# Dense layer with squared ReLU: a new order of loads and transposes in the head of the kernel

## The chip, the cores and the metric

The kernel runs on one core of a Trainium2 chip. The metric is the time of one execution on the device in microseconds, as the median of several runs. A core has a matrix engine (TensorE, called PE in the profile, with its weight loads as PEld), VectorE (DVE), ScalarE (ACT), GpSimd (POOL) and SyncE (SP), and 16 DMA engines[...]. The queues used here are those of SyncE (`nc.sync`), ScalarE (`nc.scalar`) and GpSimd (`nc.gpsimd`). SBUF is the working memory with 128 partitions; PSUM holds what TensorE writes, in eight banks.

## What is computed

Two dense layers with a squared ReLU between them, all in bfloat16:

```python
B, S, D, F = 1, 2048, 576, 4608
h = jnp.einsum("bsd,df->bsf", x, w1) + b1
r = jnp.where(h > 0, h, 0)
h = r * r
out = jnp.einsum("bsf,fd->bsd", h, w2) + b2
```

The width D = 576 is four full chunks of 128 and a rest of 64. This rest, the "tail columns" of x and the "small rows" of w1, is what makes the head of the kernel intricate.

## The kernel before

The 2048 rows of x are cut into four blocks of 512. For each block the first layer needs x transposed (the width on the partitions). Blocks 1 to 3 come transposed by DMA; block 0 is loaded as it is, in four tiles of 128 rows, and transposed by TensorE, so that work can start early. The columns of w1 are split: the first 512 (4 groups of 128, tile `w1n`, 128 rows at a time, and `w1n8` for the last 64 rows) are used in block 0 at once; the other 4096 (`w1_h`) are used in `a_rows`, in pairs of products that fill the upper and the lower half of the array with 64 rows each. For these, the transposed x (`xT`) holds every 64-row chunk in both partition halves: nine slots named `E3, O, .., SPC, E, ..`, filled by copies between the halves (`dup_windows`).

The head, in program order. First the warm-up products and the loads:

```python
wps = ps_o.tile([P, 512], FP32, name="wps", tag="po")
WARM = [512] * 6 + [128]
for i, n in enumerate(WARM):
    keep(nc.tensor.matmul(wps[:, 0:n], lhsT=ones[:, 0:P], rhs=ones[:, 0:n], start=True, stop=True))
...
def load_x(eng, rt):                                    # one tile of 128 rows, 144 KB
    keep(eng.dma_start(out=xs[:, rt, :], in_=x2[rt * P:(rt + 1) * P, :]))
def load_w1n(eng, k):                                   # 128 rows x 512 columns, 128 KB
    keep(eng.dma_start(out=w1n[:, k, :], in_=w1[k * P:(k + 1) * P, 0:GW]))
def load_w1n8(eng, h):                                  # 64 rows, 2 of the 4 groups, 32 KB
    src = w1[NK * P:D, 0:GW].rearrange("p (i h f) -> p i h f", h=2, f=P)
    keep(eng.dma_start(out=w1n8[h * H:(h + 1) * H, :, :], in_=src[:, :, h, :]))
...
load_x(nc.sync, 0)
load_x(nc.scalar, 1)
load_w1n(nc.sync, 0)
load_x(nc.scalar, 2)
load_w1n(nc.sync, 1)
load_x(nc.sync, 3)
for k in range(2, NK):                                  # NK = 4
    load_w1n(nc.sync, k)
...                                                     # b1 and b2 by GpSimd's queue
for (j0, j1) in [(0, 1), (1, 2), (2, 4), (4, 6), (6, 8), (8, 10), (10, 12)]:
    load_w1(nc.sync, 0, j0, j1)                         # w1_h: 144 KB for one j, 288 KB for two
    load_w1(nc.sync, 1, j0, j1)
    if j0 == 0:
        load_w1n8(nc.sync, 0)
        load_w1n8(nc.sync, 1)
```

Then the transposes of block 0, its copies out of PSUM, and the first products. `part(h, k)` is four products (one for each group) of chunk k with the half h of the block (256 rows). `x_transpose(j, k)` is one transpose of tile j; k = 4 (NK) is the tail, taken as the last 128 columns.

```python
for j in range(2):
    for k in range(NK):
        x_transpose(j, k)
for j in range(2):
    x_transpose(j, NK)
x_copies(0)                          # PSUM to xT: 3 by VectorE, 2 by ScalarE
part(0, 0)
for k in range(NK + 1):
    x_transpose(2, k)
part(0, 1)
part(0, 2)
for k in range(NK + 1):
    x_transpose(3, k)
x_copies(1)
dup_windows(0)                       # two copies of 64 x 2048 by VectorE
part(0, 3)
part(1, 0)
make_b1T()                           # transposes b1 and copies it
for k in range(1, NK):
    part(1, k)
...
for i in (1, 0):                     # the small rows: pairs of products of 64 rows, then ReLU
    pair(i, False, True)
    ...
```

After the head come `a_rows(0)`, where each step j has 18 products in 9 pairs and takes two new PSUM banks, and the rest of the kernel, which the change hardly touches: the first layer of block 1, the last 128 output columns for both (`phase_t`), the others (`phase_b`), and the same for blocks 2 and 3.

Of the kernel before, what the change touches and what calls it, by code (L numbers as in the profile page):

```python
# [11 lines left out]
BF16 = mybir.dt.bfloat16  # L12
FP32 = mybir.dt.float32
# [4 lines left out]
def kernel(  # L18
# [21 lines left out]
    GW = G * P  # L40
# [18 lines left out]
    wps = ps_o.tile([P, 512], FP32, name="wps", tag="po")  # L59
    ones = nc.const_aps.tensor(1.0, [P, 512], BF16)  # L60
    WARM = [512] * 6 + [128]
    for i, n in enumerate(WARM):
        keep(nc.tensor.matmul(wps[:, 0:n], lhsT=ones[:, 0:P], rhs=ones[:, 0:n], start=True, stop=True))  # L63

    xs = const.tile([P, RT, D], BF16, name="x_sb")
    w1n = wpool.tile([P, NK, GW], BF16, name="w1n")
    w1n8 = wpool.tile([P, G // 2, P], BF16, name="w1n8")
    w1_h = wpool.tile([P, NC, FH], BF16, name="w1_h")
    w1_v = w1.rearrange("(c p) f -> p c f", p=H)

    def load_x(eng, rt):
        keep(eng.dma_start(out=xs[:, rt, :], in_=x2[rt * P:(rt + 1) * P, :]))

    def load_w1n(eng, k):
        keep(eng.dma_start(out=w1n[:, k, :], in_=w1[k * P:(k + 1) * P, 0:GW]))

    def load_w1n8(eng, h):
        src = w1[NK * P:D, 0:GW].rearrange("p (i h f) -> p i h f", h=2, f=P)
        keep(eng.dma_start(out=w1n8[h * H:(h + 1) * H, :, :], in_=src[:, :, h, :]))

    def load_w1(eng, h, j0, j1):
        keep(eng.dma_start(out=w1_h[h * H:(h + 1) * H, :, j0 * P:j1 * P],
                      in_=w1_v[:, :, GW + h * FH + j0 * P:GW + h * FH + j1 * P]))

    load_x(nc.sync, 0)
    load_x(nc.scalar, 1)
    load_w1n(nc.sync, 0)
    load_x(nc.scalar, 2)
    load_w1n(nc.sync, 1)
    load_x(nc.sync, 3)  # L90
    for k in range(2, NK):
        load_w1n(nc.sync, k)

    ident = const.tile([P, P], BF16, name="ident")
    make_identity(nc, ident[:])
    b1_rows = const.tile([P, P], BF16, name="b1_rows")
    nc.gpsimd.memset(b1_rows[:], 0.0)
    nc.gpsimd.dma_start(out=b1_rows[0:NFT, :], in_=b1.rearrange("(ft p) -> ft p", p=P))
    b2_col = const.tile([P, 1], BF16, name="b2_col")
    nc.gpsimd.dma_start(out=b2_col[:], in_=b2[DM:D].rearrange("(d o) -> d o", o=1))  # L100
    b2T = const.tile([P, 1], FP32, name="b2T")
    nc.gpsimd.tensor_copy(out=b2T[:], in_=b2_col[:])
    warm = const.tile([P, 1], FP32, name="warm")
    keep(nc.scalar.activation(out=warm[:], in_=nc.const_aps.tensor(0.0, [P, 1], FP32), func=ACT.Relu))

    E3, O, SPC, E = 0, 1, 5, 6
    LO_W = [O, O + 1, O + 2, O + 3, E, E + 1, E + 2, E3, SPC]
# [30 lines left out]
    alloc_xT(0)  # L138
    xT0 = xT_blk[0]
    HS = SB // 2  # L140
    tb_po = [ps_o.tile([P, 2, HS], BF16, name="tb", tag="po") for _ in range(2)]
    tb_ph = [ps_h.tile([P, 2, HS], BF16, name="tb", tag="ph") for _ in range(4)]
    half_banks = [tb_ph, None]

    def x_transpose(j, k):
        h, q = divmod(j, 2)
        qc = slice(q * P, (q + 1) * P)
        bank, slot, c0 = (half_banks[h][k], 0, k * P) if k < NK else (half_banks[h][2], 1, D - P)
        keep(nc.tensor.transpose(bank[:, slot, qc], xs[:, j, c0:c0 + P], ident[:]))  # L149

    def x_copies(h):
        hc = slice(h * HS, (h + 1) * HS)
        for k in range(NK):
            src = half_banks[h][k][:, 0, :]
            if k % 2 == 0:
                keep(nc.vector.tensor_copy(out=xT0[:, O + k, hc], in_=src))  # L156
            else:
                keep(nc.scalar.copy(out=xT0[:, O + k, hc], in_=src))
        keep(nc.vector.tensor_copy(out=xT0[:, E3, hc], in_=half_banks[h][2][:, 1, :]))


    b1T = const.tile([P, NFT], FP32, name="b1T")

    def make_b1T():
        b1T_ps = ps_o.tile([P, P], BF16, name="b1T_ps", tag="po")
        keep(nc.tensor.transpose(b1T_ps[:], b1_rows[:], ident[:]))  # L166
        keep(nc.vector.tensor_copy(out=b1T[:], in_=b1T_ps[:, 0:NFT]))

# [26 lines left out]
    def a_full(sb, order):  # L195
        xT = xT_blk[sb]
        banks = []
        for g in range(G):
            pool, tag = (ps_o, "po") if g < 2 else (ps_h, "ph")
            banks.append(pool.tile([P, SB], FP32, name="pn", tag=tag))  # L200

        def pair(i, start, stop):
            keep(nc.tensor.matmul(banks[2 * i][:], lhsT=w1n8[0:H, i, :], rhs=xT[0:H, SPC, :],  # L203
                             start=start, stop=stop, skip_group_check=order == "k_outer"))
            keep(nc.tensor.matmul(banks[2 * i + 1][:], lhsT=w1n8[H:P, i, :], rhs=xT[H:P, E3, :],  # L205
                             start=start, stop=stop, skip_group_check=order == "k_outer"))

        def full(g, k, start, stop):
            keep(nc.tensor.matmul(banks[g][:], lhsT=w1n[:, k, g * P:(g + 1) * P], rhs=xT[:, O + k, :],  # L209
                             start=start, stop=stop))  # L210

        if order == "rows_first":
            for i in (1, 0):
                pair(i, True, False)
            for g in (2, 3, 0, 1):
                for k in range(NK):
                    full(g, k, False, k == NK - 1)
                evac_h(sb, banks[g], g)
        else:
            if order == "k_outer":  # L220
                tb_new = [ps_h.tile([P, 2, HS], BF16, name="tb", tag="ph") for _ in range(2)]
                half_banks[1] = tb_new + tb_po

                def part(h, k):
                    hc = slice(h * HS, (h + 1) * HS)
                    for g in range(G):
                        keep(nc.tensor.matmul(banks[g][:, hc], lhsT=w1n[:, k, g * P:(g + 1) * P],  # L227
                                              rhs=xT[:, O + k, hc], start=(h == 0 and k == 0), stop=False,
                                              skip_group_check=True))

                for j in range(2):
                    for k in range(NK):
# [12 lines left out]
                dup_windows(0)  # L245
                part(0, 3)
                part(1, 0)
                make_b1T()
                for k in range(1, NK):
                    part(1, k)  # L250
            else:
                for g in (2, 3, 0, 1):
                    for k in range(NK):
                        full(g, k, k == 0, False)
            for i in (1, 0):
                pair(i, False, True)
                evac_h(sb, banks[2 * i], 2 * i)
                evac_h(sb, banks[2 * i + 1], 2 * i + 1)
# [35 lines left out]
    for (j0, j1) in [(0, 1), (1, 2), (2, 4), (4, 6), (6, 8), (8, 10), (10, 12)]:  # L294
        load_w1(nc.sync, 0, j0, j1)
        load_w1(nc.sync, 1, j0, j1)
        if j0 == 0:
            load_w1n8(nc.sync, 0)
            load_w1n8(nc.sync, 1)
    load_xT(1)  # L300
    for (j0, j1) in [(12, 14), (14, 16)]:
        load_w1(nc.sync, 0, j0, j1)
        load_w1(nc.sync, 1, j0, j1)
    keep(nc.sync.dma_start(out=b2_bc[:], in_=b2.partition_broadcast(P)))
    for c in (0, 2, 1, 3):
        load_w2(c)
    load_xT(2)

# [51 lines left out]
```

## Time and profile before

| what | value |
|---|---|
| time, median of 3 runs | 291.11 us (290.89 to 291.23) |
| span of the profiled run | 289.6 us |
| TensorE busy | 285.5 us, 2027 products |
| ScalarE, VectorE busy | 96.7 us, 78.6 us |
| x tile 0: issue, landing | 0.73 us, 3.72 us |
| first transpose of x | 3.77 us |
| first product of w1_h (start of `a_rows`) | 10.29 us |

How to read it: "busy" is the time during which an engine had an instruction under way. TensorE's instructions overlap, so the step from the start of one to the start of the next is the better measure of its speed. The chain of waits goes back from the last instruction to what released it, step by step; what lies on it sets the end. A time "to landing" goes from the issue of a transfer to its last completion mark[...]. The span begins about a microsecond before the kernel's first own instructions.

### The profile page before, as it was taken

The numbers are of one execution on the slowest core, as the hardware profiler recorded it, in microseconds if no ns is written. First come the engines' busy times: TensorE is split into PE (matmuls) and PEld (weight loads), VectorE is DVE, ScalarE is ACT, GpSimd is POOL, SyncE is SP. The second block draws the span as 40 slices with busy tenths as digits, with TensorE's granted clock in tenths as the row PEclk, the third lists the DMA queues.
The fourth block names the chain that finished last, engine by engine and source line by source line (L and its number), as shares of the span: only waits on it lengthen the run. The fifth ranks groups of instructions, "written<-read, shape, count | busy, mean of one in ns | idle before, by whom it ended". The sixth has DMA issues, their size and how long they took to land.

```text
span 289.6 us, 4693 instructions
## 1 busy us (share of the span) xinstructions
PE 285.5 (99%) x2027; PEld 139.9 (48%) x2032; DVE 78.6 (27%) x176; ACT 96.7 (33%) x154; POOL 2.3 (1%) x10
## 2 busy tenths in 40 slices
PE   8999999999999999999999999999999999999996
PEld 5544444444444555555544444444444455555555
DVE  1644554444500200000015444444440001100001
ACT  2566666666500000000027666666670000000000
POOL 3000000000000000000000000000000000000000
PEclk9999999999999999999999999999999999999999
DMA  7999999400001200000000000000000110000000
GB/s 198 221 245 188 308 389 212 92 0 2 0 14 25 52 16 18 16 16 18 16 16 2 1 2 0 2 0 2 0 2 0 36 38 16 16 16 19 33 16 18
DMA packets 31605, 16.52 MB, mean 57 GB/s; under 512 B 15700, under 2 KB 31584, under 8 KB 31584
## 3 DMA queue, kind: packets, MB, share of 16 engines
q1 hardware_dynamic: 31232, 15.91, 22.3%
q10 hardware_dynamic: 288, 0.30, 0.4%
q8 instruction: 16, 0.26, 0.4%
q14 instruction: 5, 0.04, 0.0%
q0 software_dynamic: 64, 0.01, 0.0%
HBM read 11.36 MB, written 2.36 MB: 47 GB/s over the span
## 4 chain that ended last, share of the span: by engine, by line
PE 98%; DMA 1%; issue 0%; DVE 0%
PE ph L188 42%; PE po L289 38%; PE pt L270 11%; PE pn L209 4%; PE pn L227 1%; DMA x_sb<-in_x_dram 1%; PE tb L149 1%; PE ph L190 1%; PE pn L203 1%; DVE o_sb L291 0%; PE b1T_ps L166 0%; PE pn L205 0%
## 5 line engine op out<-in xcount | busy, mean ns | idle before, releaser
L190 PE MATMUL ph<-xTw,w_h 64*128 64x512 bf16 x576 | 124.6, 376 | 0.0
L188 PE MATMUL ph<-xTw,w_h 64*128 64x512 bf16 x576 | 124.6, 376 | 0.0
L289 PE MATMUL po<-w_sb,hT 128*128 128x448 bf16 (+2 forms) x612 | 109.4, 341 | 0.0
L176 ACT ACTIVATE r<-ph,b1T 128x512 bf16<-128x512 f32 x128 | 81.1, 685 | 41.6 <-PE ph L190 41.6
L188 PEld LDWEIGHTS <-w_h 64*128 64x128 bf16 x576 | 54.1, 94 | 68.3
L289 PEld LDWEIGHTS <-hT 128*128 128x128 bf16 x612 | 58.5, 98 | 51.0
L177 DVE TENSOR_TENSOR hT<-r 128x512 bf16<-128x512 bf16 x144 | 61.2, 426 | 75.9 <-ACT r L176 75.5
L190 PEld LDWEIGHTS <-w_h 64*128 64x128 bf16 x576 | 54.1, 94 | 0.0
L291 DVE TENSOR_TENSOR o_sb<-po,b_bc 128x448 bf16<-128x448 f32 (+2 forms) x17 | 10.2, 597 | 125.8 <-PE po L289 125.8
L270 PE MATMUL pt<-hT,w_sb 128*128 128x512 bf16 x142 | 31.3, 379 | 0.1
L176 ACT ACTIVATE r<-pn,b1T 128x512 bf16<-128x512 f32 x16 | 10.3, 688 | 61.0 <-PE pn L205 59.6
L270 PEld LDWEIGHTS <-w_sb 128*128 128x128 bf16 x144 | 14.1, 98 | 17.0
L273 ACT ACTIVATE oT<-pt,b2T 128x512 bf16<-128x512 f32 x4 | 2.8, 688 | 28.3 <-PE pt L270 28.3
L209 PE MATMUL pn<-xTw,w1n 128*128 128x512 bf16 x45 | 10.4, 379 | 0.4 <-issue 0.3
L209 PEld LDWEIGHTS <-w1n 128*128 128x128 bf16 x48 | 4.5, 98 | 6.0 <-issue 0.8
L227 PE MATMUL pn<-xTw,w1n 128*128 128x256 bf16 x32 | 4.6, 295 | 0.0
L63 PE MATMUL wps<-const-bfloat16-1.0 128*128 128x512 bf16 (+1 forms) x7 | 2.8, 582 | 0.8 <-PEq L344 0.8
L227 PEld LDWEIGHTS <-w1n 128*128 128x128 bf16 x32 | 3.3, 107 | 0.5
L156 DVE COPY xTw<-tb 128x256 bf16<-128x256 bf16 x4 | 1.1, 292 | 6.7 <-PE tb L149 6.7
L119 DVE COPY xTw<-xTw 64x2048 bf16<-64x2048 bf16 x4 | 2.8, 690 | 0.2
L120 DVE COPY xTw<-xTw 64x2048 bf16<-64x2048 bf16 x4 | 2.7, 687 | 0.1
L149 PE MATMUL tb<-ident,x_sb 128*128 128x128 bf16 x20 | 2.4, 288 | 0.2 <-DMA x_sb<-in_x_dram 0.2
(23 smaller groups left out, 15.2 us busy)
## 6 DMA issues: line engine op xcount, KB each, us to landing
w_sb<-in_w_dram SPq DMA_DIRECT2D x4, 1296.0 KB, 12.7
w_h<-in_w_dram SPq DMA_DIRECT2D x14, 288.0 KB, 6.2
out_dram<-o_sb SPq DMA_DIRECT2D x15, 112.0 KB, 1.7
w_h<-in_w_dram SPq DMA_DIRECT2D x4, 144.0 KB, 3.5
w1n<-in_w_dram SPq DMA_DIRECT2D x4, 128.0 KB, 3.9
out_dram<-ot SPq DMA_DIRECT2D x4, 128.0 KB, 2.0
x_sb<-in_x_dram ACTq DMA_DIRECT2D x2, 144.0 KB, 2.9
x_sb<-in_x_dram SPq DMA_DIRECT2D x2, 144.0 KB, 3.4
```

What stands on the lines that cost most here:

```text
L63: keep(nc.tensor.matmul(wps[:, 0:n], lhsT=ones[:, 0:P], rhs=ones[:, 0:n], start=True, stop=True))
L149: keep(nc.tensor.transpose(bank[:, slot, qc], xs[:, j, c0:c0 + P], ident[:]))
L176: keep(nc.scalar.activation(out=r[:], in_=bank[:], func=ACT.Relu, bias=b1T[:, ft:ft + 1], scale=1.0))
L177: keep(nc.vector.tensor_tensor(out=hTs[sb][:, ft, :], in0=r[:], in1=r[:], op=ALU.mult))
L188: keep(nc.tensor.matmul(bx[:], lhsT=w1_h[0:H, LO_C[i], jc], rhs=xT[0:H, LO_W[i], :], start=(i == 0), stop=(i == NC - 1)))
L190: keep(nc.tensor.matmul(by[:], lhsT=w1_h[H:P, UP_C[i], jc], rhs=xT[H:P, UP_W[i], :], start=(i == 0), stop=(i == NC - 1)))
L203: keep(nc.tensor.matmul(banks[2 * i][:], lhsT=w1n8[0:H, i, :], rhs=xT[0:H, SPC, :], start=start, stop=stop, skip_group_check=order == "k_o ...
L209: keep(nc.tensor.matmul(banks[g][:], lhsT=w1n[:, k, g * P:(g + 1) * P], rhs=xT[:, O + k, :], start=start, stop=stop))
L227: keep(nc.tensor.matmul(banks[g][:, hc], lhsT=w1n[:, k, g * P:(g + 1) * P], rhs=xT[:, O + k, hc], start=(h == 0 and k == 0), stop=False, s ...
L270: keep(nc.tensor.matmul(pt[:], lhsT=w2_sb[:, ft, DM:D], rhs=hT[:, ft, :], start=(i == 0), stop=(i == NFT - 1)))
L289: keep(nc.tensor.matmul(po[:, 0:d1 - d0], lhsT=hT[:, ft, jj * P:(jj + 1) * P], rhs=w2_sb[:, ft, d0:d1], start=(i == 0), stop=(i == NFT - 1)))
L291: keep(nc.vector.tensor_tensor(out=o_sb[:, d0:d1], in0=po[:, 0:d1 - d0], in1=b2_bc[:, d0:d1], op=ALU.add))
```

## The change: what it does and what it is for

- One of the six long warm-up products is gone, and the warm-up writes to the other PSUM pool.
- Tile 0 of x is loaded in two column pieces, one on each queue, so that its first transposes can start with the first piece. All four tiles of x are asked for ahead of w1. The four chunks of w1n come in three loads, two of them on ScalarE's queue.
- The small rows of w1 come once in a single load that writes the same 64 rows to both partition halves (the source is read twice), instead of two loads that each bring half of the columns.
- All 16 full transposes of block 0 stand in front, in banks that hold two chunks each; VectorE does six of the eight copies.
- The tail columns (64 wide) of two x tiles are first put side by side by GpSimd, so that one transpose serves two tiles. These two transposes stand behind chunk 1 of the first half. Four small copies then take the tails to their places, and the two large copies between the halves become one of 64 x 2048 by VectorE, one of 64 x 512 by VectorE and one of 64 x 1536 by ScalarE.
- The four accumulators of the head all lie in one PSUM pool, those of the transposes in the other.
- b1 and b2 come by the hardware queues, b2's column much later; w2 comes in three loads in place of four.

The core of the diff:

```diff
-    WARM = [512] * 6 + [128]
+    WARM = [512] * 5 + [128]
...
-    w1n8 = wpool.tile([P, G // 2, P], BF16, name="w1n8")
+    w1n8 = wpool.tile([P, GW], BF16, name="w1n8")
...
+    def load_w1n8(eng):
+        src = w1[NK * P:D, 0:GW].unsqueeze(0).broadcast_to([2, H, GW])
+        keep(eng.dma_start(out=w1n8[:, :], in_=src))
...
-    load_x(nc.sync, 0)
-    load_x(nc.scalar, 1)
-    load_w1n(nc.sync, 0)
-    load_x(nc.scalar, 2)
-    load_w1n(nc.sync, 1)
-    load_x(nc.sync, 3)
-    for k in range(2, NK):
-        load_w1n(nc.sync, k)
+    load_x(nc.sync, 0, 0, 2 * P)
+    load_x(nc.scalar, 0, 2 * P, D)
+    load_x(nc.sync, 1)
+    load_x(nc.scalar, 2)
+    load_x(nc.sync, 3)
+    load_w1n(nc.scalar, 0, 1)
+    load_w1n(nc.sync, 1, 2)
+    load_w1n(nc.scalar, 2, NK)
...
+    load_w1n8(nc.sync)
+    keep(nc.scalar.dma_start(out=b1_rows[0:NFT, :], in_=b1.rearrange("(ft p) -> ft p", p=P)))
+    xs8 = const.tile([P, RT, H], BF16, name="xs8")
+    for h in range(2):
+        keep(nc.gpsimd.tensor_copy(out=xs8[:, 2 * h:2 * h + 2, :], in_=xs[:, 2 * h:2 * h + 2, NK * P:D]))
...
-    W2CH = 9
+    W2CH = 12
...
+    def dup_windows_first():
+        keep(nc.scalar.copy(out=xT0[0:H, E:E + 3, :], in_=xT0[H:P, O:O + 3, :]))
+
+    def transpose_tails():
+        tl = ps_h.tile([P, 2, P], BF16, name="tl", tag="ph")
+        for h in range(2):
+            keep(nc.tensor.transpose(tl[:, h, :], xs8[:, 2 * h:2 * h + 2, :], ident[:]))
+        x8 = xT0.rearrange("p c (h q t) -> p c h q t", h=2, q=2)
+        for q in range(2):
+            keep(nc.vector.tensor_copy(out=x8[H:P, E3, :, q, :], in_=tl[q * H:(q + 1) * H, 0:2, :]))
+        for q in range(2):
+            keep(nc.vector.tensor_copy(out=x8[0:H, SPC, :, q, :], in_=tl[q * H:(q + 1) * H, 0:2, :]))
+        keep(nc.vector.tensor_copy(out=xT0[H:P, SPC:SPC + 4, :], in_=xT0[0:H, O:O + 4, :]))
+        keep(nc.vector.tensor_copy(out=xT0[0:H, E3, :], in_=xT0[H:P, O + 3, :]))
...
-                for j in range(2):
-                    for k in range(NK):
-                        x_transpose(j, k)
-                for j in range(2):
-                    x_transpose(j, NK)
-                x_copies(0)
+                for j in range(RT):
+                    x_transpose(j)
+                dup_windows_first()
                 part(0, 0)
-                for k in range(NK + 1):
-                    x_transpose(2, k)
                 part(0, 1)
+                transpose_tails()
                 part(0, 2)
-                for k in range(NK + 1):
-                    x_transpose(3, k)
-                x_copies(1)
-                dup_windows(0)
                 part(0, 3)
-                part(1, 0)
-                make_b1T()
-                for k in range(1, NK):
+                for k in range(NK):
                     part(1, k)
+                    if k == 1:
+                        make_b1T()
...
-        if j0 == 0:
-            load_w1n8(nc.sync, 0)
-            load_w1n8(nc.sync, 1)
```

More of the change, by code (lines that the diff above doesn't have):

```diff
@@ L57 @@
     ps_o = ctx.enter_context(tc.tile_pool(name="ps_o", bufs=4, space=PSUM))
-    wps = ps_o.tile([P, 512], FP32, name="wps", tag="po")
+    wps = ps_h.tile([P, 512], FP32, name="wps", tag="ph")
     ones = nc.const_aps.tensor(1.0, [P, 512], BF16)
-    WARM = [512] * 6 + [128]
+    WARM = [512] * 5 + [128]
     for i, n in enumerate(WARM):
@@ L66, with load_x, load_w1n @@
     w1n = wpool.tile([P, NK, GW], BF16, name="w1n")
-    w1n8 = wpool.tile([P, G // 2, P], BF16, name="w1n8")
+    w1n8 = wpool.tile([P, GW], BF16, name="w1n8")
     w1_h = wpool.tile([P, NC, FH], BF16, name="w1_h")
     w1_v = w1.rearrange("(c p) f -> p c f", p=H)
[L71 to L79, printed above, removed]
+    def load_x(eng, rt, c0=0, c1=D):
+        keep(eng.dma_start(out=xs[:, rt, c0:c1], in_=x2[rt * P:(rt + 1) * P, c0:c1]))
+    def load_w1n(eng, k0, k1):
+        src = w1[k0 * P:k1 * P, 0:GW].rearrange("(k p) f -> p k f", p=P)
+        keep(eng.dma_start(out=w1n[:, k0:k1, :], in_=src))
+    def load_w1n8(eng):
+        src = w1[NK * P:D, 0:GW].unsqueeze(0).broadcast_to([2, H, GW])
+        keep(eng.dma_start(out=w1n8[:, :], in_=src))
     def load_w1(eng, h, j0, j1):
@@ L83, in load_w1 @@
                       in_=w1_v[:, :, GW + h * FH + j0 * P:GW + h * FH + j1 * P]))
-    load_x(nc.sync, 0)
-    load_x(nc.scalar, 1)
-    load_w1n(nc.sync, 0)
+    b1_rows = const.tile([P, P], BF16, name="b1_rows")
+    nc.vector.memset(b1_rows[:], 0.0)
+    load_x(nc.sync, 0, 0, 2 * P)
+    load_x(nc.scalar, 0, 2 * P, D)
+    load_x(nc.sync, 1)
     load_x(nc.scalar, 2)
-    load_w1n(nc.sync, 1)
     load_x(nc.sync, 3)
-    for k in range(2, NK):
-        load_w1n(nc.sync, k)
+    load_w1n(nc.scalar, 0, 1)
+    load_w1n(nc.sync, 1, 2)
+    load_w1n(nc.scalar, 2, NK)
     ident = const.tile([P, P], BF16, name="ident")
     make_identity(nc, ident[:])
[L96 to L102, printed above, removed]
     warm = const.tile([P, 1], FP32, name="warm")
     keep(nc.scalar.activation(out=warm[:], in_=nc.const_aps.tensor(0.0, [P, 1], FP32), func=ACT.Relu))
+    load_w1n8(nc.sync)
[3 more added lines that the diff above has]
+        keep(nc.gpsimd.tensor_copy(out=xs8[:, 2 * h:2 * h + 2, :], in_=xs[:, 2 * h:2 * h + 2, NK * P:D]))
     E3, O, SPC, E = 0, 1, 5, 6
@@ L140, with x_transpose @@
     HS = SB // 2
[L141 to L145, printed above, removed]
+    tb = [[ps_h.tile([P, 4, HS], BF16, name="tb", tag="ph") for _ in range(2)] for _ in range(2)]
+    def x_transpose(j):
         h, q = divmod(j, 2)
-        qc = slice(q * P, (q + 1) * P)
-        bank, slot, c0 = (half_banks[h][k], 0, k * P) if k < NK else (half_banks[h][2], 1, D - P)
-        keep(nc.tensor.transpose(bank[:, slot, qc], xs[:, j, c0:c0 + P], ident[:]))
@@ L151, in x_copies @@
-    def x_copies(h):
         hc = slice(h * HS, (h + 1) * HS)
-        for k in range(NK):
[L154 to L159, printed above, removed]
-    b1T = const.tile([P, NFT], FP32, name="b1T")
+        for bank in range(2):
+            for k in range(2 * bank, 2 * bank + 2):
+                keep(nc.tensor.transpose(tb[h][bank][:, k % 2, q * P:(q + 1) * P], xs[:, j, k * P:(k + 1) * P], ident[:]))
+            for k in range(2 * bank, 2 * bank + 2) if q == 1 else ():
+                copy = nc.scalar.copy if h == 1 and bank == 1 else nc.vector.tensor_copy
+                keep(copy(out=xT0[:, O + k, hc], in_=tb[h][bank][:, k % 2, :]))
@@ L164, in make_b1T @@
     def make_b1T():
-        b1T_ps = ps_o.tile([P, P], BF16, name="b1T_ps", tag="po")
+        b1T_ps = ps_h.tile([P, P], BF16, name="b1T_ps", tag="ph")
         keep(nc.tensor.transpose(b1T_ps[:], b1_rows[:], ident[:]))
@@ L198, in a_full @@
         for g in range(G):
-            pool, tag = (ps_o, "po") if g < 2 else (ps_h, "ph")
+            pool, tag = (ps_o, "po") if g < 2 or order == "k_outer" else (ps_h, "ph")
             banks.append(pool.tile([P, SB], FP32, name="pn", tag=tag))
         def pair(i, start, stop):
-            keep(nc.tensor.matmul(banks[2 * i][:], lhsT=w1n8[0:H, i, :], rhs=xT[0:H, SPC, :],
+            keep(nc.tensor.matmul(banks[2 * i][:], lhsT=w1n8[0:H, 2 * i * P:(2 * i + 1) * P], rhs=xT[0:H, SPC, :],
                              start=start, stop=stop, skip_group_check=order == "k_outer"))
-            keep(nc.tensor.matmul(banks[2 * i + 1][:], lhsT=w1n8[H:P, i, :], rhs=xT[H:P, E3, :],
+            keep(nc.tensor.matmul(banks[2 * i + 1][:], lhsT=w1n8[H:P, (2 * i + 1) * P:(2 * i + 2) * P], rhs=xT[H:P, E3, :],
                              start=start, stop=stop, skip_group_check=order == "k_outer"))
@@ L220, in a_full @@
             if order == "k_outer":
-                tb_new = [ps_h.tile([P, 2, HS], BF16, name="tb", tag="ph") for _ in range(2)]
-                half_banks[1] = tb_new + tb_po
                 def part(h, k):
@@ L229, in part @@
                                               skip_group_check=True))
-                for j in range(2):
-                    for k in range(NK):
-                        x_transpose(j, k)
-                for j in range(2):
-                    x_transpose(j, NK)
-                x_copies(0)
+                for j in range(RT):
+                    x_transpose(j)
+                dup_windows_first()
                 part(0, 0)
-                for k in range(NK + 1):
-                    x_transpose(2, k)
                 part(0, 1)
+                transpose_tails()
                 part(0, 2)
-                for k in range(NK + 1):
-                    x_transpose(3, k)
-                x_copies(1)
-                dup_windows(0)
                 part(0, 3)
-                part(1, 0)
-                make_b1T()
-                for k in range(1, NK):
+                for k in range(NK):
                     part(1, k)
+                    if k == 1:
+                        make_b1T()
             else:
@@ L303 @@
         load_w1(nc.sync, 1, j0, j1)
+    b2_col = const.tile([P, 1], BF16, name="b2_col")
+    keep(nc.sync.dma_start(out=b2_col[:], in_=b2[DM:D].rearrange("(d o) -> d o", o=1)))
+    b2T = const.tile([P, 1], FP32, name="b2T")
+    keep(nc.gpsimd.tensor_copy(out=b2T[:], in_=b2_col[:]))
     keep(nc.sync.dma_start(out=b2_bc[:], in_=b2.partition_broadcast(P)))
-    for c in (0, 2, 1, 3):
+    for c in range(3):
         load_w2(c)
```

## The prediction

> **What bounds the kernel now.** I read the page first (busy shares), then the chain of waits over the first 11 us, then the engines' busy time by stretch, then the issues of transfers with their time to landing. The page:
>
> ```profile
> PE 285.5 (99%) x2027; PEld 139.9 (48%) x2032; DVE 78.6 (27%) x176; ACT 96.7 (33%) x154; POOL 2.3 (1%) x10
> PE 98%; DMA 1%; issue 0%; DVE 0%
> ```
>
> TensorE is busy for 99% of the span, and 98% of the chain that ended last lies on it. So only two things count: how much TensorE has to do, and when it can start. The busy time by stretch (columns: stretch, its length, then busy time and instruction count of PE, PEld, DVE, ACT, POOL, clock, DMA share, GB/s) shows where idle time is left:
>
> ```profile
> 0.00:3.77 3.77, 2.83 (x7) 0.89 (x7) 0.00 (x0) 1.49 (x2) 2.07 (x9) 1.00 0.52 153
> 3.77:9.85 6.08, 6.08 (x54) 5.24 (x55) 2.97 (x9) 1.29 (x4) 0.18 (x1) 1.00 0.83 206
> 9.85:77.00 67.15, 66.99 (x603) 30.20 (x604) 31.60 (x74) 45.26 (x72) 0.00 (x0) 1.00 0.73 173
> ```
>
> From 9.85 us on TensorE has 66.99 us of work in 67.15: nothing to win there. The change touches only what lies ahead of it, the head: 3.77 us of which the 2.83 busy ones are warm-up products that nobody uses, and 6.1 us of transposes and first products. The chain of waits, in order of time (start us, length us, what):
>
> ```profile
> 0.73 2.99 DMA x_sb<-in_x_dram
> 3.73 0.04 issue
> 3.77 1.25 PE tb L149 x10
> 5.02 0.86 PE pn L227 x4
> 5.88 0.53 PE tb L149 x5
> 6.42 0.98 PE pn L227 x8
> 7.40 0.28 PE tb L149 x5
> 7.68 0.87 PE pn L227 x8
> 8.55 0.06 PE b1T_ps L166
> 8.61 1.31 PE pn L227 x12
> ```
>
> Three readings. First, the head waits for x tile 0 until 3.72 us (0.73 + 2.99), though the last warm-up product, which the timeline starts at 3.29, has left TensorE free from about 3.4: 0.37 us idle. Second, the same instruction has two speeds. Four 256-column products take 0.86 us at 5.02 (0.215 each), twelve take 1.31 at 8.61 (0.109 each); five transposes take 0.53 (0.106) and later 0.28 (0.056). The start times in the trace put the switch at 6.5 us, inside the group of 8. Third, between 3.77 and the start of the paired products that fill the rest (first L188 product at 10.29 in the timeline) TensorE hardly waits: the head is 6.52 us of work, part of it at half speed. In fast-speed time that work is 21 transposes x 0.056 + 32 products x 0.109 + 2 row pairs x 0.216 = 1.18 + 3.49 + 0.43 = 5.10 us.
>
> [...] here the release came 5.7 us after the first warm-up product (0.78 to 6.5)[...]. [...] each issue occupies its queue for 0.40 to 0.45 us, and the DMA share is near 1 from 2.5 to 7.3 us. [...] the new w1n8 load has a source whose slowest dimension is the copy count 2[...].
>
> **The change part by part, on TensorE.**
> - *Warm-up*: one 512-column product less. They start 0.43 us apart in the timeline, so TensorE is free at about 2.97 instead of 3.40. The first product still starts at 0.78.
> - *x tile 0 in two pieces on two queues*: 64 and 80 KB side by side, instead of 144 KB beside 144 KB of tile 1. In the trace the completion marks of the two first transfers ran from 3.15 to 3.52 and from 3.33 to 3.73. With half the bytes ahead I choose 3.45 for tile 0. TensorE starts at 3.45: 0.32 us earlier. That is at half speed, so it is worth about 0.16 us.
> - *Order of loads*: all of x now goes ahead of w1, so 16 transposes stand in front. At 0.107 each: tile 0 from 3.45, tile 1 from 3.88, tile 2 from 4.31, tile 3 from 4.74 to 5.17. Before, the third and fourth transfers in issue order landed at 4.13 and 4.32 with two whole tiles ahead of them; with one tile less I put tiles 1 and 2 at 3.8 to 4.1. Tile 3 is third on the sync queue (issue about 1.65); in that place before stood w1 chunk 1, of which 12 of 16 engines were done at 4.66 and the last at 5.86. I choose 4.65, as the two small GpSimd transfers that landed between 4.1 and 5.7 are gone from there. So no wait, narrowly.
> - *Tails*: four tail transposes become two; with b1's there are 19 instead of 21. That saves 2 x 0.056 = 0.11 us.
> - The products are the same 32 + 4. New sum in fast-speed time: 1.06 + 3.49 + 0.43 = 4.98.
>
> If the switch stays at 6.5: from 3.45 to 6.5 lie 3.05 us at half speed, worth 1.52. Left are 4.98 - 1.52 = 3.46, so the paired products start at 6.5 + 3.46 = 9.96 instead of 10.29: **0.33 us less**.
>
> **What runs beside it, and its slack.** DVE: each PSUM copy of 128x256 follows the one before by 0.22 us (4 of half 0 done by about 5.2, 2 of half 1 by 5.8; ScalarE does the other two by 6.2). Then the tail transposes, at about 6.75; their four small copies from 7.05 take some 0.9, the 64x2048 copy 0.69 (row of L120), one 64x512 copy about 0.2, b1T 0.2: done at 9.05, 0.9 us before it is needed. ScalarE's 64x1536 copy: from 128x256 (0.373) and 128x512 (0.685) I get 1.22 ns a column, so 1.9 us, done near 8.1. Two GpSimd copies of the tail columns: an estimate of 0.3 us each (its 128x128 affine select took 0.29), done by 5.3. w1 chunks: 1088 KB of x and w1 in all, landed at 7.05 before with other things between; chunk 0 is needed at 5.17, chunk 1 at 6.0, chunks 2 and 3 at 6.8. That fits. The b2 load, the w2 loads in thirds and the PSUM pools lie far from any wait.
>
> What does not fit easily is w1n8. It is issued near 3.55, once the second piece of tile 0 has landed; the two loads it replaces were issued from 5.05 on. If it runs on two engines, each has 64 packets of 1024 bytes; the trace's packet records give 46 ns for one, so 2.94 us, behind the x and w1 packets which end near 5.1 to 5.5. It lands at about 8.6: in time for its use at 9.5. But the w_h transfers queue behind it on those two engines: 36 packets of 256 bytes at 18 ns (0.65 us) each for the first four, 36 of 512 bytes at 27 to 39 ns (1.0 to 1.4 us) for the next. That gives 9.3 and 10.0 for the first pair (needed at 9.96), 10.9 and 11.6 for the second (needed at 11.9), 12.8 and 14.0 for the third (needed at 13.85). So I expect waits of 0 to 0.5 us, and choose 0.18.
>
> Sum: 291.11 - 0.33 + 0.18 = **290.96**; I say 290.95.
>
> **The rivals.**
> - *The two-engine load becomes the bound.* [...] Against: 0.4 to 1 us of slack in two of three places. Full size if the packets are slower, as those between 4 and 5 us were (70 to 80 ns for 1024 bytes): w1n8 at 10 or later, every stage 1 us later, 291.7 or more.
> - *All sixteen engines take it after all.* Then there is no wait and the time is 290.75.
> - *Tile 3 arrives late*, at 5.9 as the third transfer on sync did before. TensorE stands for up to 0.7 us before its transposes; at half speed that costs 0.35: 291.2 to 291.3. [...]
> - *The transfer was hidden anyway.* If the warm-up switch moves with the start of real work or varies from run to run, an earlier start buys nothing but the 0.11 us of the tails. The three times before (290.89 to 291.23) already spread as far as my gain.
>
> **Range and chances.** Lower end: everything in time and x earlier than I think, or the switch earlier: 290.3. Upper end: late w_h or a late tile 3, 291.7. Two per cent are 5.8 us, more than half of the head: no part of this reaches it except by something unforeseen.
>
> **What would show it.** First transpose near 3.45; 16 transposes without a gap until 5.2; fast products from 6.5; first paired product (L188 before) near 9.96 to 10.1. The rival on the two engines shows as a w1n8 landing far later than the 2.5 to 3 us of before[...], and as waits of TensorE on w_h between 10 and 14 us. A wait on x between 4.3 and 5.2, or products at 0.215 after 7 us, would make the prediction wrong in the other ways named.

## The result and the profile after

The changed kernel takes **292.55 us** (292.24 to 292.87, 6 runs) against 291.06 for the kernel before: a ratio of 1.0051, 95% interval 1.0038 to 1.0064. It is 1.5 us longer, not a little shorter, and lies above the stated range (290.3 to 291.7).

The page says that TensorE still carries the end, and that something else has joined the chain:

```profile
PE 284.8 (98%) x2029; PEld 138.7 (48%) x2029; DVE 79.3 (27%) x181; ACT 97.4 (34%) x153; POOL 1.5 (1%) x9
PE 96%; DMA 3%; SPq 0%; DVE 0%; issue 0%
```

In the views below, `x_sb` is x, `w_h` is w1_h, `w1n` is both w1n and w1n8, `b_rows` are the rows of b1, `wps` is the warm-up, `tb` and `tl` are the transposes of x, `pn` the products of the head and `ph` the paired products.

The busy time by stretch shows that the loss is in the head and nowhere else. In the second row TensorE is busy for 3.94 us, where it was busy for all 6.08 before; after 9.85 us it is full again:

```profile
0.00:3.77 3.77, 2.79 (x10) 1.13 (x10) 0.11 (x1) 1.14 (x1) 0.70 (x6) 1.00 0.51 130
3.77:9.85 6.08, 3.94 (x38) 3.06 (x38) 3.51 (x12) 2.46 (x5) 0.58 (x2) 1.00 0.68 196
9.85:20.00 10.15, 10.07 (x93) 4.86 (x95) 4.45 (x11) 6.73 (x12) 0.00 (x0) 1.00 1.15 235
20.00:77.00 57.00, 57.00 (x516) 25.60 (x513) 26.63 (x62) 37.52 (x61) 0.19 (x1) 1.00 0.69 165
```

The chain of waits over the head names the wait (start us, length us, what):

```profile
1.19 2.74 DMA x_sb<-in_x_dram
3.92 0.05 issue
3.97 0.28 PE tb L149 x2
4.25 5.64 DMA b_rows<-in_b_dram
9.89 0.05 issue
9.93 0.23 PE b1T_ps L173
10.16 0.87 PE pn L231 x8
```

A load of 9 KB, the rows of b1, is under way from 4.25 to 9.89. TensorE's timeline shows what this costs (start us, length us, instruction, count, idle time before it and what ended it):

```profile
3.97 0.64 PE L149 MATMUL tb<-ident,x_sb 128*128 128x128 bf16 x8 [0.40 <-DMA x_sb<-in_x_dram]
5.26 0.40 PE L149 MATMUL tb<-ident,x_sb 128*128 128x128 bf16 x4 [0.65 <-DMA x_sb<-in_x_dram]
...
9.93 0.23 PE L173 MATMUL b1T_ps<-ident,b_rows 128*128 128x128 bf16 x1 [1.37 <-DMA b_rows<-in_b_dram]
...
11.41 0.38 PE L195 MATMUL ph<-xTw,w_h 64*128 64x512 bf16 x1
```

Three idle spells: for x tile 1, for x tile 3, and 1.37 us for b1. The first paired product, at 10.29 before, now starts at 11.41. This start alone accounts for the profiled runs: 291.46 - 10.29 = 281.17 and 292.56 - 11.41 = 281.15. (They lie 1.1 us apart and not 1.5, since the profile of the kernel before is of one of its longest executions.) In the runs below the same difference stays between 281.1 and 281.4, except where TensorE waits again right after it (281.6, b1 moved) or its clock falls back (282.6, the single load alone). So one number tells nearly all of it: when the paired products start.

Why would 9 KB take 5.6 us? The times of the completion marks in the trace tell it. The load of x tile 3 leaves 16 of them, from 4.37 to 5.22; others:

| transfer in the kernel after | most marks | the last two |
|---|---|---|
| small rows of w1 (w1n8; 3 records) | one at 4.15 | 8.79, 9.71 |
| b1's rows (13 records) | one at 5.09, ten by 6.89 | 9.07, 9.89 |
| w_h, first / second transfer | by 7.11 / 7.77 | 9.40, 10.29 / 9.82, 10.71 |
| w_h, third transfer | by 9.49 | 10.42, 11.15 |

The w1n8 load leaves two late marks, and b1's rows and the next three w_h loads issued after it are late on exactly two marks each, b1's by 2.2 and 3.0 us (6.89 against 9.07 and 9.89). That these marks stand for two of the DMA engines, the same two each time, is the reading that fits; the records of the marks don't name the engine.

### The profile page after: what moved, and what is told of

Same layout as the page of the kernel before. It is cut to its first block, busy times and chain, and to the rows that moved or that the text cites. A ratio compares the mean times of both kernels' runs of the same rounds, so it can differ in the third digit from the quotient of the medians.

```text
span 290.6 us, 4700 instructions
## 1 busy us (share of the span) xinstructions
PE 284.8 (98%) x2029; PEld 138.7 (48%) x2029; DVE 79.3 (27%) x181; ACT 97.4 (34%) x153; POOL 1.5 (1%) x9
## 4 chain that ended last, share of the span: by engine, by line
PE 96%; DMA 3%; SPq 0%; DVE 0%; issue 0%
PE ph L195 42%; PE po L285 38%; PE pt L266 11%; PE pn L216 4%; DMA b_rows<-in_b_dram 2%; DMA x_sb<-in_x_dram 1%; PE ph L197 1%; PE pn L210 1%; PE pn L231 0%; SPq L72 0%; DVE o_sb L287 0%; PE tb L149 0%; PE b1T_ps L173 0%; PE pn L212 0%
## 5 line engine op out<-in xcount | busy, mean ns | idle before, releaser
L216 PE MATMUL pn<-xTw,w1n 128*128 128x512 bf16 x48 | 10.9, 379 | 0.0
L231 PE MATMUL pn<-xTw,w1n 128*128 128x256 bf16 x32 | 4.0, 273 | 0.0
L149 PE MATMUL tb<-ident,x_sb 128*128 128x128 bf16 x16 | 1.6, 242 | 1.1 <-DMA x_sb<-in_x_dram 1.1
L210 PE MATMUL pn<-xTw,w1n 64*128 64x512 bf16 x8 | 2.4, 379 | 0.0
L212 PE MATMUL pn<-xTw,w1n 64*128 64x512 bf16 x8 | 2.4, 379 | 0.0
```

Source lines behind the costliest of these rows:

```text
L210: keep(nc.tensor.matmul(banks[2 * i][:], lhsT=w1n8[0:H, 2 * i * P:(2 * i + 1) * P], rhs=xT[0:H, SPC, :], start=start, stop=stop, skip_grou ...
```

## The experiments

Theory: the load with the leading dimension 2 occupies two engines, and b1, w1n8 and w_h come late one behind the other. Rivals: b1's place on its queue; reading the same rows twice; the new order of loads; the shortened warm-up. Each time is a median. Ratio and 95% interval compare all executions with those of the kernel before on the same chip (medians 290.90 to 290.96), so the ratio is not the quotient of the two medians.

**Two loads instead of one.**

```diff
-        src = w1[NK * P:D, 0:GW].unsqueeze(0).broadcast_to([2, H, GW])
-        keep(eng.dma_start(out=w1n8[:, :], in_=src))
+        for h in range(2):
+            keep(eng.dma_start(out=w1n8[h * H:(h + 1) * H, :], in_=w1[NK * P:D, 0:GW]))
```

> The changed kernel with one edit: the small rows of w1 come in two loads of 64 partitions each, the same bytes from the same rows of w1, in the place of the one load whose source has the copy count 2 as its slowest dimension. Theory (two engines: the single load runs on 2 of the 16 DMA engines, and all that queues behind it there comes late, b1 first): w1n8 lands by about 7.3, b1's rows by about 6.9, the transpose of b1 no longer waits, the paired products start at 9.7 to 9.9 instead of 11.57, and the time falls by about 1.7 us to 290.8. Rival (b1 is late because it stands last on ScalarE's queue behind two w1 loads): b1 still lands near 9.9 and the time stays at 292.5. Rival (reading the same rows twice is slow in itself): w1n8 still lands after 9, the time stays above 292.

Measured: 291.62 us, ratio 1.0035 (1.0022 to 1.0049). The marks of w1n8 end at 6.95 and 7.16, all those of b1 by 7.38, and the wait for b1 is gone. Both rivals about b1's place and about reading twice fall: neither was changed here. But the paired products start at 10.52, not at 9.7 to 9.9, the time falls by 0.9 us and not by 1.7, and the kernel is still longer than the one before. TensorE's timeline:

```profile
4.22 0.62 PE L149 MATMUL tb<-ident,x_sb 128*128 128x128 bf16 x8 [0.46 <-DMA x_sb<-in_x_dram]
5.47 0.40 PE L149 MATMUL tb<-ident,x_sb 128*128 128x128 bf16 x4 [0.63 <-DMA x_sb<-in_x_dram]
...
6.75 0.61 PE L231 MATMUL pn<-xTw,w1n 128*128 128x256 bf16 x4 [0.45 <-DMA w1n<-in_w_dram]
```

It waits twice for x and once for chunk 1 of w1, which lands at 6.70. Something else is in the times: of 22 executions 8 lie between 292.7 and 293.6 (I call them, and their like in other runs, the late group), the other 14 at 292.1 or less. None of the 51 executions of the kernel before that were taken beside the last experiments is above 291.51.

**Only b1 moved.**

```diff
-    keep(nc.scalar.dma_start(out=b1_rows[0:NFT, :], in_=b1.rearrange("(ft p) -> ft p", p=P)))
+    keep(nc.gpsimd.dma_start(out=b1_rows[0:NFT, :], in_=b1.rearrange("(ft p) -> ft p", p=P)))
```

> The changed kernel with one edit: b1's rows come by GpSimd's queue, as in the kernel before, issued near 1.5; the single w1n8 load stays. Theory (two engines, several late arrivals one behind the other): b1 lands near 5.4 and its wait is gone, but w1n8 still lands at 9.7 and the second w_h transfer at 10.7, so TensorE waits there instead; paired products without a stop only from about 10.7, time about 291.7, some 0.8 us less than 292.5. Rival (only b1's place on its queue was wrong): the whole loss comes back and the time is 290.7 to 290.9.

Measured: 292.23 us, ratio 1.0043 (1.0027 to 1.0058). b1 lands at 4.73. In the profile the next late transfer takes over, as expected: the first product of the upper half waits for the second w_h transfer, whose two late marks are at 9.91 and 10.46. The chain, after the small rows:

```profile
10.25 0.21 PE ph L195
10.47 0.04 issue
10.51 0.39 PE ph L197
```

The rival (all comes back) is out. The median fell by 0.3 us where I expected 0.8; 7 of 13 executions again lie at 292.2 or above.

**The single load alone, in the kernel before.** The two w1n8 loads become the one of the change, at the same place.

```diff
-            load_w1n8(nc.sync, 0)
-            load_w1n8(nc.sync, 1)
+            load_w1n8(nc.sync)          # source as in the change
```

> The kernel before with one part of the change alone: its two w1n8 loads become the single load with the copy count 2 in front, at the same place of the queue (behind the first two w_h transfers); the products read the same rows from the new places. b1 comes by GpSimd's queue early. Theory (two engines): w1n8 lands at 10 to 10.6 instead of by 8.2, after it is needed (9.85), and the next w_h transfers lag on two engines; paired products start at 10.7 to 11.2 instead of 10.29, time up by 0.4 to 0.9 us to 291.5 to 292. Rival (the single load is harmless; the loss is from b1's place or from the order of x and w1): time within 0.2 us of the kernel before.

Measured: 294.08 us, ratio 1.0108 (1.0088 to 1.0129): the theory's direction, at more than three times the size. The chain shows the load itself, issued at 5.03, as the wait:

```profile
5.03 6.78 DMA w1n<-in_w_dram
11.82 0.05 issue
11.86 0.45 PE pn L203
```

And the busy time by stretch, cut at the marks of the granted clock, shows what I had not counted (the column before the last two is the clock):

```profile
5.23:8.65 3.42, 3.11 (x33) 2.50 (x32) 1.22 (x4) 0.65 (x2) 0.18 (x1) 1.00 0.74 182
8.65:12.06 3.41, 1.29 (x13) 0.85 (x12) 1.07 (x3) 0.00 (x0) 0.00 (x0) 1.00 0.68 177
12.06:15.47 3.41, 3.41 (x18) 1.23 (x16) 1.70 (x4) 2.42 (x4) 0.00 (x0) 0.50 0.99 246
```

TensorE stood still for over 2 us, the stretch held 1.29 us of work in 3.41, and for the next 3.41 us the clock was 0.50. (Such a stretch of 3.41 us is a window in what follows.) Here a wait was paid once as a wait and once more at half speed. By their mean clock (0.993 and 0.994) this happened in two more of the six executions; the other three kept a clock of 1.000 and took 293.3 to 293.8, so the wait without the fallback costs 2.4 to 2.9 us.

**The leading 2 without reading twice.** The single load takes its two blocks of 64 rows from two places of w1, so the lower partitions hold other rows than the reference needs and the output differs.

```diff
-        src = w1[NK * P:D, 0:GW].unsqueeze(0).broadcast_to([2, H, GW])
+        src = w1[6 * H:9 * H, 0:GW].rearrange("(a q) f -> a q f", q=H)[0:3:2, :, :]
```

> The changed kernel, but the single w1n8 load takes its two blocks of 64 rows from two places of w1 (rows 384 to 447 for the lower partitions, rows 512 to 575 for the upper), so the source has the leading dimension 2 and no row is read twice; the lower half thus holds other rows than the reference needs. Theory (the leading dimension of 2 confines the load to two engines): again [...]the last two at 8.5 to 10, b1 as late as 9.5 to 10, time 292.3 to 292.9. Rival (reading the same rows twice, with step 0, is what is slow): sixteen marks together by 7.5, b1 by 7, time about 1 us less.

Measured, in a single execution: 291.81 us; again three records for the load, one at 4.11 and two at 8.94 and 9.21, and b1 at 9.12. The leading dimension of 2 does it without any row being read twice. The chain:

```profile
4.14 4.98 DMA b_rows<-in_b_dram
9.12 0.05 issue
9.17 0.23 PE b1T_ps L173
```

It ends 0.77 us earlier than with the repeated rows (9.12 against 9.89), and the time lies below the 292.3 to 292.9 that I expected. A single execution doesn't tell whether that is the repetition or chance, so the repetition may have a share in the size of the wait, though not in its kind.

**The warm-up and the late group.** With two w1n8 loads, the sixth long warm-up product is put back (`[512] * 5` to `[512] * 6`).

> As the run with two w1n8 loads, and the sixth long warm-up product is put back. Tile 0's first piece lands at 2.88, so this product holds TensorE until about 3.40 and the first transposes come 0.43 us later, at 3.40. Theory (the first transposes are not on the path that sets the end, because TensorE then waits for tile 1 at 3.92 and tile 3 at 5.22 anyway): within 0.2 us of the run with five, paired products start at the same 9.7 to 9.9. Rival (the earlier end of the warm-up shortens the head): 0.3 to 0.4 us slower than with five. Rival ([...]the sixth product helps to keep the array busy): as fast or faster, with the switch earlier.

Measured: 291.38 us, ratio 1.0015 (1.0006 to 1.0025), and only 1 of 22 executions in the late group instead of 8. Work that nobody uses made the kernel shorter by 0.24 us at the median. This is the third of the three expectations (the product keeps the array busy); its second half, an earlier switch to full speed, can't be read from two profiles, since the switch falls at 6.31 in this one and at 4.06 in the one with five. TensorE's idle time in the head, though, went from 1.54 us to 0.33. The same edit the other way, in the kernel before (the windows and the 70 per cent in the expectation are a reading of the profiles' clock records and busy times; the table further below has them):

> The kernel before with one warm-up product less, nothing else. TensorE then stands still from about 2.97 to 3.72, when tile 0 lands. Theory C (windows): an execution whose window ends between 3.2 and 4.0 no longer reaches some 70 per cent and switches a window later; that is about a quarter of them, each 1 to 1.5 us longer, so the mean rises by 0.2 to 0.4 us and the spread grows. Rival (the sixth product is idle work whose end at 3.40 is hidden behind the load): time the same within 0.1 us.

Measured: 290.92 us, ratio 0.9996 (0.9987 to 1.0005). My estimate of 0.2 to 0.4 us was wrong: in the kernel before, the sixth product is hidden. In the profile the array has work from 3.56 us on without a gap, and none of the 13 executions is above 291.42.

**The old order of loads with the rest of the change.** Chunks of w1 between the x tiles again, interleaved transposes, w1n8 in two loads at its old place, b1 by GpSimd, five warm-up products; and the same with eight.

```diff
     load_x(nc.sync, 0, 0, 2 * P)
     load_x(nc.scalar, 0, 2 * P, D)
-    load_x(nc.sync, 1)
+    load_w1n(nc.sync, 0, 1)
+    load_x(nc.scalar, 1)
...                                  # w1 chunk 1, x 2, x 3, chunks 2 and 3; TensorE as before
```

> What the runs so far point to: tile 0 in two pieces, shared tail transposes and five warm-up products are kept; w1 chunks go between the x tiles again as in the kernel before, TensorE interleaves as before, w1n8 comes in two loads behind the first w_h pair, b1 by GpSimd's queue. Theory A (order of loads and the two-engine load are the loss, the other parts are a small gain): no wait of more than 0.3 us on TensorE after 4.2, paired products at 9.3 to 10.0, time 290.3 to 290.9, at or below the kernel before (290.9). Rival (the tails' longer chain of copies, or GpSimd's part in it, costs time): 291.2 or more, with TensorE waiting for VectorE or GpSimd before the paired products.

> The run with the old order of loads, with eight long warm-up products instead of five. They hold TensorE until about 4.26, so tile 0, there at 3.1, is transposed 1.1 us later than with five, and TensorE has no idle spell before 4.3. Theory C (a window of 3.41 us releases the full speed if TensorE was busy for more than a share between 0.70 and 0.77 of it; with five products the window that ends near 6.7 holds only 0.64 and the release comes at 10.2): the slower group of that run (8 of 13 executions at 292.3 to 293.6) vanishes, all executions between 290.6 and 291.5, median 290.9 to 291.1 instead of 292.5. Rival (the slower group comes from transfers or something else, and the earlier transposes are worth their time): the slower group stays, and the faster one is 0.2 to 0.5 us later.

Measured: 292.52 us, ratio 1.0034 (1.0015 to 1.0053), with five; 291.51, ratio 1.0018 (1.0010 to 1.0025), with eight. With five, 8 of 13 executions lie between 292.3 and 293.6, with eight none of 21 (the longest is 291.99). The other five with five products lie between 290.7 and 291.1, near the 290.3 to 290.9 that Theory A had expected of all. The profile with five happened to be one of the late ones, and its chain shows them from within:

```profile
4.47 0.41 PE tb L149 x2
...
6.69 1.71 PE pn L231 x8
8.39 0.43 PE tb L149 x4
8.82 0.21 PE tl L162 x2
9.03 1.49 PE pn L231 x8
10.52 0.06 PE b1T_ps L173
10.58 1.31 PE pn L231 x12
```

Eight products take 1.71 us, at 0.214 each, as late as 6.7 to 8.4; the full speed comes at 10.16. In the profile with eight the same eight products take 0.87:

```profile
0.78 3.68 PE wps L63 x9
4.45 0.65 PE tb L149 x6
...
6.07 0.22 PE tb L149 x4
6.29 0.87 PE pn L231 x8
```

The trace records when the granted clock changes; I call the switch to full speed the release. In all 13 profiles that hold such records (the one with the old order and eight products has none) the stretches from one change to the next are multiples of 3.41 us (3.40 to 290.12 in the profile after is 84 of them, 6.51 to 289.82 before is 83, the 3.41 us at 0.50 with the single load alone are one), and their phase differs from run to run (a release at 3.40 in the profile after, at 4.06 with two w1n8 loads). Cutting the head into such windows back from the release gives the table (busy: TensorE's recorded time over 3.41 us):

| kernel | window ending at release | the window before it |
|---|---|---|
| before | 3.10 to 6.51: 0.95 | up to 3.10: 0.68 |
| after | up to 3.40: 0.77 | empty |
| old order, five warm | 6.75 to 10.16: 1.00 | 3.34 to 6.75: 0.75; up to 3.34: 0.75 |

A window at 0.75 (put at 0.64 in the expectation above) was not followed by the release, and one at 0.77 was. With two w1n8 loads one at 0.88 was (2.99 us of work up to the release at 4.06); in the kernel before the one at 0.68 was not. The recorded times run over by modelled ends, so I hold only to "about three quarters", for these profiles. To keep the full speed took less: in the profile after it stayed through windows at 0.69 (3.40 to 6.82) and 0.60 (6.82 to 10.23), while the window at 0.38 in the run with the single load alone lost it, and so did one at 0.38 at the very end of the profile after (286.71 to 290.12).

By an estimate from these shares the idle spells of the new order can push a window too low. With two w1n8 loads, a window that holds both waits for x (0.46 and 0.63 us) is by that run's profile busy for at most 2.32 of 3.41 us, which is 0.68; an execution whose windows fall that way would run up to one more window of 3.41 us at half speed, worth up to 1.7 us. That the late executions of the other runs are of this kind is inferred from their times: only the one late profile shows it, and the mean clock doesn't tell (it is 1.000 there too). The late group is no simple function of the idle time either: with 0.33 us of it in the profile, 1 of 22 executions is late; with 1.54, 8 of 22; with 0.86, 8 of 13.

My other estimate for eight, a median of 290.9 to 291.1, was too low: the longer warm-up is itself on the chain, until 4.45, and the executions lie about 0.5 us above the five that with five products are not late. The rival's second half was right there.

**Filling the gaps between the transposes.** Two 512-column products nobody uses, behind tile 0's and tile 2's transposes, with two w1n8 loads:

> The run with two w1n8 loads, and two products of 512 columns that nobody uses, one behind tile 0's transposes and one behind tile 2's, where TensorE otherwise stands still (0.67 and 0.79 us). The output is the same. Theory C (the switch to full speed comes at the end of a free window of 3.41 us in which the array was busy for more than some 70 per cent; the idle spells make some executions miss a window and pay up to 1.7 us): the slower group of that run (8 of 22 executions at 292.7 to 293.6) shrinks to at most 1 in 10, and the median falls from 291.6 to 291.2 or 291.4, although TensorE has more to do. Rival (the idle spells are only lost time): no change of the slower group, median equal or up to 0.4 us higher.

Measured: 291.79 us, ratio 1.0044 (1.0025 to 1.0063), with 6 of 16 executions above 292.5 and two of them at a mean clock of 0.994, as in the run where the clock fell back. The expectation failed. The profile is of a good execution (release at 4.08), so why these two products don't help stays open, and this run speaks against the windows as the only cause of the late group.

**What is left without late windows: the order of loads.**

> The changed kernel with two w1n8 loads and eight long warm-up products instead of five; all of x still ahead of w1, 16 transposes in front. Theory C: the slower group (8 of 22 with five products) vanishes. Theory A (what is left is the order of loads: chunks 1 to 3 of w1 land at 6.5 to 7 with most of the products behind them): the rest stays 0.3 to 0.6 us above the kernel before, median 291.2 to 291.5. Rival (only the windows made that version longer than before): median equal to the kernel before within 0.1 us, 290.9 to 291.0.

> The run with two w1n8 loads, and on TensorE the old interleaving: transposes of tiles 0 and 1, the products of chunk 0, tile 2, chunks 1 and 2, tile 3, the tails, the rest; the loads keep the new order (all of x ahead of w1). Theory A (the new order of loads costs time: with w1 behind x, no product can run while x is still coming): the interleaving alone wins nothing, since chunk 0 lands at 5.2 and chunk 1 near 6.5 and tile 3's transposes now stand behind chunk 1; time within 0.3 us of 291.6. Rival B (the 16 transposes in front cost it): 0.4 to 0.8 us faster, 290.8 to 291.2.

> As near to the kernel before as the shared tails allow: tile 0 whole on the sync queue, tile 1 on ScalarE's, w1 chunks between, six long warm-up products, interleaved transposes, w1n8 in two loads behind the first w_h pair, b1 by GpSimd's queue; kept of the change are the shared tail transposes with their copies, the PSUM pools, b2 and w2. If those parts do what they are for (two transposes of 0.056 us less), 0.05 to 0.15 us less than the kernel before, 290.8 to 290.9, no slower group. Rival (the longer chain of copies behind the tails delays the paired products): 0.2 us or more above the kernel before.

Measured: with eight warm-up products and all of x first, 291.49 us, ratio 1.0028 (1.0014 to 1.0041), 2 of 22 late (293.85 and 294.54), so the late group nearly vanishes. With the old interleaving on TensorE but the new loads, 293.15 us, ratio 1.0060 (1.0038 to 1.0082), 5 of 7 late; that is no gain, so the 16 transposes in front are not what costs, but it is also far above what Theory A allowed. With the old loads of x and w1, six warm-up products and of the change only the tails, the copies, the pools and the later b2 and w2: 290.97 us, ratio 1.0002 (0.9993 to 1.0010), none of 13 late.

So what the single load does not account for lies in what this last run takes back together: the order of the loads, tile 0 in two pieces, five warm-up products in place of six, and the places of w1n8 and b1. The traces point to the order. Chunk 1 of w1 lands at 5.6 to 6.7 us in the eight profiles with all of x ahead of w1 and at 5.1 to 5.9 in the six others. No run changes the order alone, and these runs don't split its plain waits from its late windows to better than 0.3 us. The shared tails, kept in the last run, bring nothing that can be measured.

No version beat the kernel before.

## Why the prediction was wrong

- **The sum missed b1.** The prediction put b1's copy into VectorE's line ("b1T 0.2: done at 9.05") but asked of no load except w1n8 and w_h whether it needs the two engines. b1's rows do, by their marks: two of them came at 9.07 and 9.89, TensorE waited 1.37 us, and this set the start of the paired products. This is the term that failed: "waits of 0 to 0.5 us, and choose 0.18". The mechanism was named, and its two engines agree with the two late marks; the wait that counted was on another transfer. Splitting the load brought the start of the paired products from 11.41 to 10.52.
- **The two-engine load was sized too small.** "It lands at about 8.6" was 9.71, and the first w_h pair, "9.3 and 10.0", came at 10.29 and 10.71. The packet time of 46 ns held for most packets; but from 6.06 to 7.00 us these packets start 0.042 us apart, and from 7.00 to 8.42 0.021 us apart, as if one of the two engines had done nothing for the load for about 1 us. What it did instead is not shown. With b1 moved away, the late second w_h transfer still held TensorE to 10.51.
- **The gain of 0.33 us was not there.** It rested on the switch to full speed staying at 6.5. The release moves from run to run: 3.40 in the profile after, 6.51 before, 10.16 in another. The profile of the kernel before was one of its longer runs (291.46, where its median is 291.06), so I took an unfavourable release for the rule. "If the switch stays at 6.5" was stated and not questioned far enough. Even a release at 4.06 did not help: with two w1n8 loads the paired products started at 10.52, 0.23 us later than before, as TensorE waited 0.46, 0.63 and 0.45 us for tile 1, tile 3 and chunk 1 of w1 ("That fits" was said of these chunks). The sum was also too large from the start: its parts, 0.16 for the earlier tile 0 and 0.11 for the tails, make 0.27; the 0.33 sets a calculated 9.96 against a measured 10.29.
- **"Tile 3: I choose 4.65"** was 5.22, with 0.65 us idle; and tile 1 cost 0.40 where I had none. Tile 0 came earlier than I thought (2.88 and 3.04, first transpose at 2.97 instead of 3.45), which only made the following wait longer. The rival "tile 3 arrives late" was right in kind. A release one window late, as in the profile with the old order and five products (10.16), is probably what the two-load version suffers in 8 of 22 executions; no profile of these shows it.
- **Right**: the two engines, an assumption that nothing in the trace of before showed (the two late marks at 8.79 and 9.71 fit it); VectorE, ScalarE and GpSimd in time (VectorE done at 8.92 without b1, GpSimd's copies 0.29 us each, ScalarE's 64x1536 copy 1.47 us); nothing after the head changes; nothing near 2%.
- **Small slips that carry no weight**: an issue takes 0.40 to 0.45 us for most x and w1n loads, but 0.61 to 0.73 for w1n8 and w_h in the same trace; and at 0.65 us each the second w_h pair would come at 10.6 and 11.3, not 10.9 and 11.6 (measured 11.15 and 11.65).

## What to carry to other kernels

Look at the slowest dimension of the source of every load: here a 2 there (w1n8) left two marks at 8.79 and 9.71, and two loads of 64 rows in its place ended at 6.95 and 7.16. Then look at everything that is queued behind such a load: the victim is whichever of them is needed first (here b1's rows, 1.37 us of waiting, then w_h, and in the kernel before the load itself). In the first microseconds of a kernel, compare orders by many executions and by the time of release to full speed (3.40 to 10.16 us in these profiles), not by one profile; of the version with two loads, 8 of 22 executions were late. Where work can't start anyway, a longer warm-up can pay (six products in place of five: 0.24 us at the median with two w1n8 loads), but one that outlasts the first load is paid for (eight with the old order: about 0.5 us more than the executions with five that were not late).

## What I had not expected of the hardware

- b1's packets were issued on another queue than w1n8's, and 30 of the 36 passed between 5.9 and 6.3. The last six, by the late marks (9.07 and 9.89) those on w1n8's two engines, passed only at 8.51 to 8.56 and 9.32 to 9.38, just after the starts of w1n8's packets went from 0.021 us apart to 0.042 (8.42) and after the last of them (9.19). In the run with other rows the last six passed at 8.25 to 8.58, one for one between w1n8's last packets. So packets of a small transfer on another queue stood for 2.2 us (6.3 to 8.51) here while w1n8's packets passed, and in the other run passed in turn with them; what decides is not shown.
- The clock fell back quickly: with the single load alone, one stretch of 3.41 us with 1.29 us of recorded work was followed by 3.41 us at 0.50. In the profile after it stayed up through windows at 0.69 and 0.60.
